# An attention and gated-MLP kernel on one core: the first pair of weight blocks is loaded behind the second unit's queries, keys and values

## The chip, the cores and the metric

The program runs on 1 core of one Trainium2 chip. The metric is device time in microseconds (us), the median of the runs of one kernel. Engines are named as in the profile: PE is the matrix engine, PEld its weight loads, DVE the vector engine, ACT the scalar engine, POOL the GpSimd engine, SP the engine that issues every DMA of this kernel.

## The reference, cut to what matters

```python
# attention inside chunks of 64 tokens; q, k, v are (8 batches, 8 heads, 576, 64)
scores = scale * q_c @ k_c.T;  attn = softmax(scores);  out = attn @ v_c
# the heads side by side give x: 4608 tokens x 512
xn  = x / sqrt(mean(x * x) + 1e-6) * rms_g
g   = xn @ w_gate                    # 512 -> 1536
val = xn @ w_val                     # 512 -> 1536
return (silu(g) * val) @ w_out       # 1536 -> 512
```

All arrays arrive as float32 in the reference; the three weights are handed to the kernel as 64-bit integer words of wider numbers and are turned into float32 on the chip.

## The kernel before

**Work.** Tokens are cut into 18 units of 256 (`UT`), two units to a token tile of 512 (`TT`), 9 tiles. Attention is done unit by unit, in two halves of 128 tokens each: scores (`scores`, L254), softmax on DVE and ACT (`softmax`, L267 to L271; `softmax_rows`, L288 to L303), a transpose of the probabilities on PE (`att_transpose`, L312, copied back by ACT in L313), the product with the values (`att_values`, L430) and the scaling by row sums and by the RMS (`norm`, L452, L440, L441, L443, L458). The normed rows are transposed on PE (L511) and split by ACT (L489) and DVE (L490) into a high and a low part, `xh` and `xl`, so that three matmuls with rounded operands make one product of float32 accuracy.

**Weights.** The hidden dimension is cut into 12 blocks, f0 to f11. The list `pairs` holds 18 loads of 1 MB, in the order up f0, up f1, out f0 and f1, up f2, up f3, out f2 and f3, and so on; here they are called block 0, block 1, block 2 and so on. An "up" load carries the gate and the value weights of one f, an "out" load the output weights of two. Each is loaded as raw 64-bit words (`conv_load`, L159) and converted: ACT takes the high words (L167) and the low words (L168); DVE clamps, shifts, merges and adds (L176, L177, L178, L181); ACT makes the rounded high half (L192), DVE the low half (L200), both in a tile `parts`; an up block is also stored as float32 (`wfd`, L194) when L181 is done. There are three working tiles `w` for this, so block 6 takes the tile of block 3 and waits for block 3's L200.

**Stages.** Units 0 and 1 are done first, with PE mostly waiting; then token tile 0 runs through the 12 blocks (L522 is the up product, `ps_g` and `ps_v`; L557 the product with the output weights, `acc`), while the 18 loads are converted under it and the attention of units 2 and 3 is put between. From the second tile on the weights are there, and in the last six tiles products of halves are combined with fewer matmuls (L736, L912).

**Order.** The order on each engine through the first token tile is not written out: the framework's scheduler chooses it, once, when the program is built, from the order in which the code calls things and from priorities. From the second tile on the order on PE is the one written. Each engine works through its list in order; a list entry that waits holds up all behind it. SP issues the DMAs in its own list order, and a DMA also waits until the one eight places ahead of it has landed. The PSUM pool `ps_a` has two banks: unit 2's scores take both (`ps_s_555`, `ps_s_556`), and the transposes of its probabilities (L312) need these banks again, so the first L312 waits until ACT has read all of the one bank and the second until it has read all of the other.

`load_first_unit` loads queries and keys of unit 0 in four pieces, `load_first_values` its values, `load_unit(1)` the queries, keys and values of unit 1 (L222 to L224). The call that the change moves is at L997:

Of the kernel before, what the change touches and what calls it, by code (L numbers as in the profile page):

```python
# [78 lines left out]
def tile_chunk_attn_swiglu(  # L79
# [76 lines left out]
    def conv_load(n):  # L156
        if n < len(pairs):
            kind, f = pairs[n]
            nc.sync.dma_start(raws[n], w_up[f] if kind == "up" else w_out[f // 2])  # L159
# [58 lines left out]
    def load_unit(u):  # L218
        qt = io.tile([P, NPAIR, UT], F32, tag="io", name="qt")
        kt = io.tile([P, NPAIR, UT], F32, tag="io", name="kt")  # L220
        vt = io.tile([P, NPAIR, UT // CH, D], F32, tag="io", name="vt")
        nc.sync.dma_start(qt, qT[u])  # L222
        nc.sync.dma_start(kt, kT[u])
        nc.sync.dma_start(vt, v[u])  # L224
        for s in range(2):
            state[2 * u + s] = {"q": qt, "k": kt, "v": vt}

    def load_first_unit():

        qt, kt = (x[:, 2 * i : 2 * i + 2].rearrange("p s (a t) -> p (s a) t", t=UT) for i in range(2))  # L230
        for s in range(2):
            part = slice(s * P, (s + 1) * P)
            nc.sync.dma_start(qt[:, :, part], qT[0][:, :, part])
            nc.sync.dma_start(kt[:, :, part], kT[0][:, :, part])
            state[s] = {"q": qt, "k": kt}

    def load_first_values():
        vt = io.tile([P, NPAIR, UT // CH, D], F32, tag="io", name="vt")
        nc.sync.dma_start(vt, v[0])
        for s in range(2):  # L240
            state[s]["v"] = vt
# [752 lines left out]
            self.n += 1  # L994

    load_first_unit()
    conv_load(0)  # L997
    load_first_values()
    load_unit(1)
    nc.sync.dma_start(g_col, rms_g)  # L1000
    for n in range(1, AHEAD):
        conv_load(n)
# [216 lines left out]
```

## Time and profile before

| | us |
|---|---|
| runs of the kernel | 924.17, 926.05, 926.56; median 926.05 |
| the profiled execution: its own time, and its span | 923.97, 922.2 |
| PE busy | 897.4 (97%) |
| DVE, ACT, POOL busy | 571.3, 449.3, 171.4 |
| first matmul of the first token tile | at 35.58 |

The span is the stretch from the first to the last recorded instruction. A row of the timeline gives the start, the duration, the engine, the line, what is written and read, and in brackets how long the engine had been idle before it and what ended that. Rows of one line that follow each other are merged, with their count behind x.

### The profile page before, as it was taken

The numbers are of one execution on the slowest core, as the hardware profiler recorded it, in microseconds if no ns is written. First come the engines' busy times: TensorE is split into PE (matmuls) and PEld (weight loads), VectorE is DVE, ScalarE is ACT, GpSimd is POOL, SyncE is SP. The second block draws the span as 40 slices with busy tenths as digits, with TensorE's granted clock in tenths as the row PEclk, the third lists the DMA queues.
The fourth block names the chain that finished last, engine by engine and source line by source line (L and its number), as shares of the span: only waits on it lengthen the run. The fifth ranks groups of instructions, "written<-read, shape, count | busy, mean of one in ns | idle before, by whom it ended". The sixth has DMA issues, their size and how long they took to land.

```text
span 922.2 us, 17497 instructions
## 1 busy us (share of the span) xinstructions
PE 897.4 (97%) x6900; PEld 735.5 (80%) x6900; DVE 571.3 (62%) x985; ACT 449.3 (49%) x721; POOL 171.4 (19%) x155
## 2 busy tenths in 40 slices
PE   5699999999999999999999999999999999999998
PEld 4578788888888788888878888888888888888886
DVE  5989975464546555864764735657555545544775
ACT  4989953463446553654444424546433332332352
POOL 0000002233200000233233002323330003432200
PEclk9999999999999999999999999999999999999999
DMA  8699899777975643888798788676997965785901
GB/s 336 263 331 345 320 347 347 244 264 230 306 275 148 185 150 114 310 283 298 231 352 309 283 332 318 219 261 224 328 332 260 343 241 182 284 298 191 354 24 68
DMA packets 101969, 242.84 MB, mean 263 GB/s; under 512 B 9344, under 2 KB 64128, under 8 KB 86912
## 3 DMA queue, kind: packets, MB, share of 16 engines
q1 hardware_dynamic: 101888, 241.74, 74.6%
q8 instruction: 54, 0.88, 0.4%
q14 instruction: 27, 0.22, 0.1%
HBM read 176.69 MB, written 65.01 MB: 262 GB/s over the span
## 4 chain that ended last, share of the span: by engine, by line
PE 84%; ACT 6%; DVE 5%; DMA 3%; issue 1%; SPq 1%; POOL 0%; ACTq 0%; DVEq 0%
PE acc L557 22%; PE ps_c L736 11%; PE ps_b L736 10%; PE ps_a L736 10%; PE ps_g L522 8%; PE ps_v L522 7%; PE ps_d L736 5%; PE ps_o L376 2%; PE ps_s L254 2%; PE ps_b L912 2%; PE ps_c L912 2%; PE ps_a L912 2%; DMA wr<-wsd 1%; ACT e L294 1%; PE ps_d L912 1%
## 5 line engine op out<-in xcount | busy, mean ns | idle before, releaser
L557 PE MATMUL acc<-wo,gh 128*128 128x512 f32 x384 | 118.5, 390 | 0.0
L736 PE MATMUL ps_c<-xp,wr 128*128 128x512 f32 x432 | 104.5, 391 | 0.2 <-DMA wr<-wsd 0.2
L736 PE MATMUL ps_b<-xp,wr 128*128 128x512 f32 x432 | 104.7, 391 | 0.0
L736 PE MATMUL ps_a<-xp,wr 128*128 128x512 f32 x432 | 103.5, 390 | 0.0
L522 PE MATMUL ps_g<-xh,parts 128*128 128x512 f32 x288 | 96.8, 396 | 0.3 <-ACT xh L489 0.3
L522 PE MATMUL ps_v<-xh,parts 128*128 128x512 f32 x288 | 95.1, 391 | 0.0
L736 PEld LDWEIGHTS ps_c<-xp,wr 128*128 128x128 f32 x432 | 80.7, 188 | 17.5 <-DMA wr<-wsd 0.7
L736 PEld LDWEIGHTS ps_a<-xp,wr 128*128 128x128 f32 x432 | 80.9, 188 | 16.9
L736 PEld LDWEIGHTS ps_b<-xp,wr 128*128 128x128 f32 x432 | 80.6, 188 | 17.1
L557 PE MATMUL acc<-parts,gh 128*128 128x512 f32 x288 | 90.2, 394 | 0.0
L809 POOL TENSOR_TENSOR g<-u,u 128x512 f32<-128x512 f32 x18 | 23.2, 1288 | 328.8 <-DVE u L805 270.2
L557 PEld LDWEIGHTS acc<-wo,gh 128*128 128x128 f32 x384 | 71.9, 188 | 15.0
L838 ACT CAST gh<-g 128x512 fp32r<-128x512 f32 x64 | 39.8, 623 | 80.6 <-PE acc L557 64.4
L839 DVE TENSOR_TENSOR gl<-g,gh 128x512 fp32r<-128x512 f32 x64 | 45.0, 706 | 54.9 <-ACT gh L838 54.8
L557 PE MATMUL acc<-wo,gl 128*128 128x512 f32 x192 | 75.0, 390 | 0.0
L522 PEld LDWEIGHTS ps_g<-xh,parts 128*128 128x128 f32 x288 | 54.1, 189 | 12.7 <-ACT xh L489 0.7
L522 PEld LDWEIGHTS ps_v<-xh,parts 128*128 128x128 f32 x288 | 54.5, 189 | 11.3
L557 PEld LDWEIGHTS acc<-parts,gh 128*128 128x128 f32 x288 | 53.3, 188 | 11.3
L544 DVE TENSOR_TENSOR sg<-ps_v,sg 128x512 f32<-128x512 f32 x36 | 24.7, 687 | 52.6 <-PE ps_v L522 40.4
L557 PE MATMUL acc<-parts,gl 128*128 128x512 f32 x144 | 56.4, 392 | 0.0
L522 PE MATMUL ps_v<-xl,parts 128*128 128x512 f32 x144 | 56.4, 392 | 0.0
L522 PE MATMUL ps_g<-xl,parts 128*128 128x512 f32 x144 | 56.3, 391 | 0.0
(165 smaller groups left out, 1593.2 us busy)
## 6 DMA issues: line engine op xcount, KB each, us to landing
wr<-wsd SPq DMA_DIRECT2D x63, 1024.0 KB, 8.9
wo<-wod SPq DMA_DIRECT2D x24, 1024.0 KB, 8.5
raw<-w_up_dram SPq DMA_DIRECT2D x12, 1024.0 KB, 8.1
vt<-v_dram SPq DMA_DIRECT2D x18, 512.0 KB, 6.9
wsd<-parts SPq DMA_DIRECT2D x18, 512.0 KB, 7.4
qt<-qT_dram SPq DMA_DIRECT2D x17, 512.0 KB, 5.8
kt<-kT_dram SPq DMA_DIRECT2D x17, 512.0 KB, 6.0
out_dram<-o SPq DMA_DIRECT2D x28, 256.0 KB, 2.3
```

The costliest lines, as they stand in the source:

```text
L254: nc.tensor.matmul(st["s"][j][c * CH : (c + 1) * CH, pr], st["q"][rows, pr, tok : tok + CH], st["k"][rows, pr, tok : tok + CH], start=True ...
L294: nc.scalar.activation(e[:, pr, j], st["s"][j][:, pr], AF.Exp, scale=SCALE, bias=mx[:, j, s, pr], accum_out=rs[:, s, pr, j],)
L376: nc.tensor.matmul(st["o"][(2 * c + t) * Q : (2 * c + t + 1) * Q, h * D : (h + 1) * D], eT[c][rows, t, h], vt[rows, c, h], start=True, sto ...
L522: nc.tensor.matmul(ps, a[f][:, cols], b[dt], start=(dt == 0 and i == 0), stop=(dt == NDT - 1 and i == 2),)
L544: nc.vector.tensor_tensor(sg, pv, sg, op=ALU.mult)
L557: nc.tensor.matmul(acc[s], a[:, cols], b, start=(f == 0 and i == 0), stop=(f == NF - 1 and i == 2),)
L736: nc.tensor.matmul(ps, w[:, a, m, cols], xp[:, b, kt], start=start and kt == 0 and i == 0, stop=stop and kt == 1 and i == 2, skip_group_ch ...
L809: nc.gpsimd.tensor_tensor(g[:, 0, 1], kp["u2"], kept[0]["u2"], op=mult)
L838: nc.scalar.copy(gh, src)
L839: nc.vector.tensor_tensor(gl, src, gh.bitcast(F32), op=ALU.subtract)
L912: nc.tensor.matmul(ps[m][INTO[p]], w[:, m, a], parts[c], start=p in FROM and i == 0 and k == 0, stop=p in LAST and i == NPR - 1 and k == 2 ...
```

## The change

One call is moved two lines down, behind `load_first_values()` and `load_unit(1)`:

```diff
     load_first_unit()
-    conv_load(0)
     load_first_values()
     load_unit(1)
+    conv_load(0)
     nc.sync.dma_start(g_col, rms_g)
     for n in range(1, AHEAD):
         conv_load(n)
```

On SP, at the start of the program, the load of block 0 (L159, `raw`) goes from the fifth DMA to the ninth:

```order
 L233 DMA x<-qT_dram 128x4x128
 L234 DMA x<-kT_dram 128x4x128
-L159 DMA raw<-w_up_dram 128x1024
 L239 DMA vt<-v_dram 128x1024
 L222 DMA qt<-qT_dram 128x1024
 L223 DMA kt<-kT_dram 128x1024
 L224 DMA vt<-v_dram 128x1024
+L159 DMA raw<-w_up_dram 128x1024
 L1000 DMA g_col<-rms_g_dram 128x4
 L159 DMA raw<-w_up_dram 128x1024
```

Four DMAs of 512 KB now stand ahead of that load. The scheduler answers by another order on PE, DVE, ACT and SP through the whole first token tile. On DVE, in the first unit's attention, three instructions of block 0's conversion (L176 to L178) stood between the softmax sums (L278) and the scaling of the first half (L452):

```order
-L176 TENSOR_SCALAR w<-w 128x1024
-L177 TENSOR_SCALAR w<-w 128x1024
-L178 SCALAR_TENSOR_TENSOR w<-raw,w 128x1024
 L452 TENSOR_TENSOR x<-ps_o_255,rs 128x4x2x32
 L452 TENSOR_TENSOR x<-ps_o_256,rs 128x4x2x32
-L181 ISA w<-raw,w 128x2048
```

They now follow behind the softmax reductions of unit 1, some seventeen rows further down the list.

Later on DVE, where unit 2's scores are reduced (L288) and block 3's low half is made (L200), the order before was:

```order
L181 ISA w<-raw,w 128x2048
L200 TENSOR_TENSOR parts<-w,parts 128x1024
L288 TENSOR_REDUCE mx_u<-ps_s_555 128x8
L544 TENSOR_TENSOR sg<-ps_v,sg 128x512
L288 TENSOR_REDUCE mx_u<-ps_s_556 128x8
```

and with the change it is:

```order
L181 ISA w<-raw,w 128x2048
L288 TENSOR_REDUCE mx_u<-ps_s_555 128x8
L288 TENSOR_REDUCE mx_u<-ps_s_556 128x8
L200 TENSOR_TENSOR parts<-w,parts 128x1024
L289 TENSOR_SCALAR mx_u<-mx_u 128x16
```

Block 3's low half now stands behind both reductions.

On ACT, in the softmax of unit 2 (L294, exponentials of `ps_s_555` and `ps_s_556`, 16 of them), two function tables are used in turn, one for L294 and one for the SiLU of the blocks (L540). From the first SiLU in that stretch (block f2) to block 5's high half (L192) the order before was:

```order
L540 ACT_TABLE_LOAD
L540 ACTIVATE sg<-ps_g 128x512
L294 ACT_TABLE_LOAD
L294 ACTIVATE e,rs_u<-ps_s_556,mx_u 128x64 x3
L545 CAST gh<-sg 128x512
L294 ACTIVATE e,rs_u<-ps_s_556,mx_u 128x64
L294 ACTIVATE e,rs_u<-ps_s_555,mx_u 128x64 x4
L294 ACTIVATE e,rs_u<-ps_s_556,mx_u 128x64 x4
L192 CAST parts<-w 128x1024
```

and with the change, from behind the first SiLU on, it is:

```order
L294 ACTIVATE e,rs_u<-ps_s_555,mx_u 128x64
L545 CAST gh<-sg 128x512
L294 ACTIVATE e,rs_u<-ps_s_555,mx_u 128x64 x2
L294 ACTIVATE e,rs_u<-ps_s_556,mx_u 128x64 x4
L294 ACTIVATE e,rs_u<-ps_s_555,mx_u 128x64 x4
L540 ACT_TABLE_LOAD
L540 ACTIVATE sg<-ps_g 128x512
L294 ACT_TABLE_LOAD
L294 ACTIVATE e,rs_u<-ps_s_556,mx_u 128x64 x2
L545 CAST gh<-sg 128x512
L294 ACTIVATE e,rs_u<-ps_s_556,mx_u 128x64 x2
L192 CAST parts<-w 128x1024
```

A second SiLU (block f3), with a table load on either side, now stands inside the softmax, ahead of the last four exponentials and of block 5's high half. On PE the second L312 of unit 2 moves from the middle of f3's products to behind them.

## Rows read from the trace of the kernel before

**Rows 1.** The page, busy time of PE, share, instructions.
```profile
PE 897.4 (97%) x6900; PEld 735.5 (80%) x6900; DVE 571.3 (62%) x985; ACT 449.3 (49%) x721; POOL 171.4 (19%) x155
```
**Rows 2.** Waits of PE over the span: us in total, times, longest.
```profile
PE ps_s L254 <- DMA x<-kT_dram: 6.7, 2, 5.0
...
PE ps_o L376 <- DMA eT<-away_e: 1.6, 2, 1.4
...
PE ps_t L312 <- ACT e L294: 1.0, 2, 0.5
```
**Rows 3.** Busy time by stretch: length, then each engine, clock granted, DMA.
```profile
50.00:75.00 25.00, 24.49 (x169) 19.83 (x168) 22.58 (x31) 23.45 (x54) 0.00 (x0) 1.00 0.95 336
75.00:125.00 50.00, 49.48 (x335) 39.99 (x334) 48.85 (x67) 44.98 (x83) 3.62 (x2) 1.00 0.92 336
```
**Rows 4.** DMA issues from 0 to 5.5 us: KB, us to landing.
```profile
raw<-w_up_dram SPq DMA_DIRECT2D x1, 1024.0 KB, 7.2
...
kt<-kT_dram SPq DMA_DIRECT2D x1, 512.0 KB, 9.5
```
**Rows 5.** Timeline of SP at the start.
```profile
3.44 0.62 SPq L159 DMA_DIRECT2D raw<-w_up_dram  x1
...
5.05 0.74 SPq L223 DMA_DIRECT2D kt<-kT_dram  x1
```
**Rows 6.** Timeline of all engines, first unit.
```profile
12.18 0.69 DVE L176 TENSOR_SCALAR w<-w 128x1024 f32<-128x1024 f32 x1
...
12.68 1.14 PE L430 MATMUL ps_o<-vt,eT 64*64 64x64 f32 x32 [0.40 <-ACT eT L313]
...
13.63 1.23 DVE L178 SCALAR_TENSOR_TENSOR w<-raw,w 128x1024 int32<-128x1024 int32 x1
14.78 0.75 DVE L452 TENSOR_TENSOR x<-ps_o,rs 128x256 f32<-128x256 f32 x2
15.34 0.55 PE L430 MATMUL ps_o<-vt,eT 64*64 64x64 f32 x5 [1.53 <-DVE x L452]
```
**Rows 7.** Timeline of all engines, end of the first two units.
```profile
29.02 0.55 POOL L443 TENSOR_TENSOR ri<-ss,mhalf 128x1 f32<-128x1 f32 x1 [9.13 <-DVE ss L441]
...
32.07 1.29 POOL L443 TENSOR_TENSOR ri<-ss,mhalf 128x1 f32<-128x1 f32 x1 [2.50 <-DVE ss L441]
...
33.40 0.72 ACT L458 ACTIVATE x<-x,ri 128x512 f32<-128x512 f32 x1
...
35.58 0.79 PE L522 MATMUL ps_g<-xh,parts 128*128 128x512 f32 x1 [0.29 <-ACT xh L489]
```
**Rows 8.** Timeline of DVE, block 3's low half and unit 2's scores.
```profile
49.01 1.21 DVE L200 TENSOR_TENSOR parts<-w,parts 128x1024 fp32r<-128x1024 f32 x1
50.15 0.68 DVE L288 TENSOR_REDUCE mx_u<-ps_s 128x8 f32<-128x512 f32 x1
```
**Rows 9.** Timeline of ACT, softmax of unit 2.
```profile
50.26 1.14 ACT L167 ACTIVATE w<-raw 128x1024 f32<-128x1024 f32 x1
...
53.38 1.28 ACT L294 ACT_TABLE_LOAD   x1 [1.31 <-DVE mx_u L289]
...
55.99 1.28 ACT L540 ACT_TABLE_LOAD   x1
57.28 0.60 ACT L540 ACTIVATE sg<-ps_g 128x512 f32<-128x512 f32 x1
...
63.20 1.11 ACT L192 CAST parts<-w 128x1024 fp32r<-128x1024 f32 x1
```
**Rows 10.** Timeline of PE, units 2 and 3 in the first token tile.
```profile
62.24 0.66 PE L312 MATMUL ps_t<-ident,e 128*128 128x128 f32 x4 [0.51 <-ACT e L294]
...
67.59 0.62 PE L557 MATMUL acc<-parts,gh 128*128 128x512 f32 x2
...
72.02 0.39 PE L522 MATMUL ps_g<-xh,parts 128*128 128x512 f32 x1
...
106.30 0.66 PE L312 MATMUL ps_t<-ident,e 128*128 128x128 f32 x4 [0.52 <-ACT e L294]
```

## The prediction

> **What bounds the kernel now.** I read the page first: PE is busy for 897.4 of 922.2 us [rows 1]. Next the waits of PE over the whole span: the large ones lie ahead of the first token tile, where PE waits for the first queries and keys; after that the longest is 1.4 us in all the rest, and the transposes of the probabilities (L312) wait for ACT's exponentials twice, 0.5 us each [rows 2]. So from 35.58 us, the first matmul of the first token tile [rows 7], PE goes nearly without a gap to the end. The time is the moment at which this dense run starts, plus the matmuls, which the change does not touch, plus the waits inside the run. Then busy time by stretch, to see which engine could make such waits: between 50 and 125 us DVE is busy 22.58 of 25 and 48.85 of 50 us, ACT 23.45 of 25 and 44.98 of 50 [rows 3]. There the weights are converted under the matmuls, with almost nothing to spare. Work that these two engines do later than before stays late until the conversion is over. That is the side on which the change can lose; the first 35 us are the side on which it can win.
>
> **The transfers.** Nothing is added or removed; one load of 1 MB passes four of 512 KB on SP's queue. Before, block 0 is issued at 3.44 and lands 7.2 us later, at 10.64; the keys of unit 1 are issued at 5.05 and land after 9.5, at 14.55 [rows 4, 5]. Three loads of 512 KB lie between these two landings, 1.5 MB in 3.9 us, so 2.6 us per MB. Unit 1's keys gain the 1 MB that went ahead and land at about 11.9; block 0 has 2 MB more ahead of it and lands at about 15.8. The loads behind are ahead of the same bytes as before: 0.
>
> **The first two units.** Before, PE finished the first half's values at 12.68 + 1.14 = 13.82, but the scaling L452 began only at 14.78, since DVE was busy from 12.18 with block 0's clamp, shift and merge (L176 to L178); unit 1's scores stood on PE behind a matmul that waited 1.53 us for that L452 [rows 6]. Without block 0 on DVE L452 can follow the values at once: 1.0 us earlier, and some 1.4 if ACT's copy of the probabilities, which had ACT's L167 ahead of it, comes earlier too. The keys at 11.9 are then no hindrance. Little of this survives: block 0's two ACT instructions (1.1 us each, as the L167 of [rows 9]) and its DVE instructions, which had filled waits before, now stand between here and the dense run, in front of unit 1's own work. One of the two on ACT takes most of the 1.4; I keep 0.35 us at the last squares, an estimate. A second piece comes from POOL. Its power for the RMS took 0.55 us at 29.02 and 1.29 us at 32.07, where DVE ran L176 and L177 beside it, and the last scaling L458 waited for it until 33.40 [rows 7]. In the new order DVE has L178 there. At 0.55 us this gives 0.74 more. I take the dense run 1.1 us earlier, at 34.5; the ends are 0.35 and 1.4.
>
> [...] No row here shows POOL beside L178, and 1.29 against 0.55 only shows that something on DVE blocks it.
>
> **The converter falls behind.** By the order, DVE had done three L178 and two L200 when it came to the second unit's low parts (L490); now it has done two and one. That is 1.23 + 1.21 = 2.4 us of work [rows 6, 8] that now lies under the dense run. It starts 1.1 us earlier, so the conversion is 1.3 us late on the clock. Then block 3's low half (L200, which ended at 50.2) has two reductions of 0.68 us ahead of it that stood behind it: 50.2 + 1.3 + 1.4 = 52.9 [rows 8]. PE waited for nothing here before, and wants this half at about 52.5 now: a wait between 0 and 1.0 us, I take 0.45.
>
> **Unit 2's softmax.** ACT's first instruction on block 6 (L167) began at 50.26, at the end of that L200, since block 6 takes block 3's working tile [rows 8, 9]; it now starts at about 53.0. What is queued behind it on ACT is the whole softmax of unit 2. From that L167 to block 5's L192 it was 63.20 - 50.26 = 12.9 us; the wait of 1.31 us in it goes, since the reductions now come first; and a SiLU with two table loads comes in, 1.28 + 0.60 + 1.28 = 3.2 us [rows 9]. So L192 begins, and the last exponential ends, at 53.0 + 12.9 - 1.3 + 3.2 = 67.8, 4.6 us later than before. The second L312 on PE waits for that exponential. It now stands behind block f3, whose products ended at 67.59 with both L312 and a wait of 0.51 in them [rows 10]: 67.59 - 0.65 (the lead left) - 0.5 - 0.4 (one L312) = 66.0. PE waits 1.8 us in place of 0.5. Behind it come the products with block 5, which want its high half (67.8 + 1.1) and its low half (another 1.2): 70.1, with about 1 us of matmuls done in between. Before, those products and the values of unit 2 took 72.02 - 67.59 = 4.4 us [rows 10]; f4 starts at 70.1 + 3.4 = 73.5, against 72.02: 1.5 us late.
>
> [...]
>
> **Unit 3's softmax.** ACT and DVE have no room to recover [rows 3], so ACT is still about 4.6 us late there and PE 1.5. Before, PE already waited 0.52 us at 106.30 [rows 10]. If the transposes stood where they were, PE would lose the other 3.1 us; but both now stand behind all products of the block before, and the first of them needs only one bank's exponentials. Between 0 and 3.1 I take 1.0, as most of the difference is covered by these products. Behind that the blocks' weights are ahead of PE again.
>
> **The sum**, as lag against the profiled execution: start -1.1, block 3 +0.45, the transpose of unit 2 +1.3, block 5 +0.85, unit 3 +1.0: **+2.5 us**. That is 926.5 on the profile's own 923.97; the median of the runs lies 2.1 us above that execution, so I forecast 926.05 + 2.5 = **928.5**. With the ends of all terms: no new wait and the full lead, -1.4, or 924.6; the least lead and the larger waits, about +5, or 931.
>
> **Rivals.**
> - *The lead survives.* If ACT reaches the SiLU of f3 as soon as its products are done, the transposes wait no more than now, and only the earlier start counts: -1.1, **924.9**, not slower. For it: the 1.53 us wait of PE and DVE's block 0 ahead of L452 are plain in the rows [rows 6], and what I lose comes from a chain of small lags. Against it: ACT has 3.2 us more ahead of the last exponentials, whatever the lag, and it decides as soon as more than 0.5 us of the wait is left. It falls at the second L312 of unit 2. Chance 0.20.
> - *More is lost.* POOL's power stays at 1.29 us, so that the run starts at 35.2, and unit 3's wait is nearer 3 than 1: 2.5 + 0.7 + 1.3 = +4.5, **930.5**. For it: DVE busy 48.85 of 50 us [rows 3]. Against it: PE, itself late, asks later. Chance 0.20.
> - *Nothing that counts.* The conversion had margin that I don't see, the waits only change places, and the start gives back what they cost: **926.0**. For it: before, PE waits in the whole tile only for the two transposes. Chance 0.15. A change that doesn't do what it says is excluded by the order on SP.
>
> **Numbers.** The forecast has 0.45. About 0.3%, 2.8 us, is what a measurement of this kernel can tell from no change: faster is below 923.3, slower above 928.8. Of the forecast, with an error of some 1.2 us, four tenths lie above; of the second rival nearly all. Slower 0.40, same 0.54, faster 0.06. The range is 924.5 to 931.0; the forecast's own is 927 to 930.
>
> **What will show it.** Right: L452 of the first half near 13.4 us; the first L522 near 34.5; a wait of PE for block 3's L200 near 53; a wait of PE for L294 of 1 to 2 us near 67; f4 near 73.5. Wrong: no wait of PE over 0.6 us between 35 and 125 us, or a first L522 at 35.5 or later; both upset the sum, the one downwards, the other upwards.

## The result, and the profile after

| | before | after |
|---|---|---|
| runs beside each other | 923.92 to 926.56, median 924.2 (5 runs) | 928.59 to 930.83, median 929.54 (5 runs) |
| profiled execution, and its span | 923.97, 922.2 | 928.81, 927.0 |
| f0, f4 and f9 start on PE (first L522) | 35.58, 72.02, 117.97 | 34.49, 75.77, 122.75 |

The changed kernel takes 1.005 times as long, 95% interval 1.0034 to 1.0065: **slower by about 5 us**. The forecast was +2.5 us, 928.5, with a range of 924.5 to 931.0. It was reckoned from 926.05, and the runs beside it had 924.2: the time came out 1.0 us from the forecast, but the change, +5.3, is more than double the +2.5.

The page of after, busy time of each engine [rows 1]:

```profile
PE 899.9 (97%) x6900; PEld 736.2 (79%) x6900; DVE 570.1 (61%) x985; ACT 452.2 (49%) x723; POOL 170.3 (18%) x155
```

The waits of PE over the span of after (in total, times, longest) [rows 2]:

```profile
PE ps_t L312 <- ACT e L294: 3.5, 2, 2.1
...
PE ps_g L522 <- DVE parts L200: 0.4, 1, 0.4
...
PE acc L557 <- ACT parts L192: 0.3, 1, 0.3
```

The transposes, which waited 1.0 us in all, wait 3.5, and two waits for halves of converted weights are new. Busy time by stretch in after [rows 3] (PE, PEld, DVE, ACT, POOL, then the clock granted to PE, the share of the DMA engines, GB/s):

```profile
35.50:50.00 14.50, 14.50 (x116) 11.68 (x114) 13.71 (x18) 12.77 (x16) 0.00 (x0) 0.87 0.76 269
50.00:75.00 25.00, 22.19 (x157) 17.06 (x150) 19.43 (x26) 21.90 (x51) 0.00 (x0) 0.93 0.99 359
75.00:125.00 50.00, 48.56 (x348) 39.25 (x339) 47.14 (x62) 45.97 (x82) 1.61 (x1) 1.00 0.91 319
```

Between 50 and 75 us PE stands still for 2.8 us, and DVE, one of the two full engines there, now has 5.6 us to spare: it waits too. The clock is below 1.00 twice. Where the time was lost is in PE's own rows of after, from block 3 to f9 [rows 10]:

```profile
53.97 0.74 PE L522 MATMUL ps_g<-xh,parts 128*128 128x512 f32 x2 [0.42 <-DVE parts L200]
...
69.11 0.66 PE L312 MATMUL ps_t<-ident,e 128*128 128x128 f32 x4 [2.10 <-ACT e L294]
70.05 2.50 PE L557 MATMUL acc<-parts,gh 128*128 128x512 f32 x5 [0.28 <-ACT parts L192]
72.34 0.63 PE L557 MATMUL acc<-parts,gl 128*128 128x512 f32 x1
72.77 0.63 PE L557 MATMUL acc<-parts,gh 128*128 128x512 f32 x1
73.20 0.50 PE L557 MATMUL acc<-parts,gl 128*128 128x512 f32 x1
73.54 0.39 PE L557 MATMUL acc<-parts,gh 128*128 128x512 f32 x1
...
111.35 0.66 PE L312 MATMUL ps_t<-ident,e 128*128 128x128 f32 x4 [1.44 <-ACT e L294]
```

Behind the wait of 2.10 us products come about 0.43 us apart, eight steps in 3.49 us from 70.05 to 73.54, not 0.227 as elsewhere; the clock granted to PE from 70 to 72 us is 0.50. At 0.227 they would have taken 1.82, so 1.67 us went there. And ACT's rows in unit 2's softmax in after [rows 9]:

```profile
54.00 1.16 ACT L167 ACTIVATE w<-raw 128x1024 f32<-128x1024 f32 x1 [1.33 <-DVE mx_u L289]
55.17 1.28 ACT L294 ACT_TABLE_LOAD   x1
...
56.90 1.28 ACT L540 ACT_TABLE_LOAD   x1
...
58.80 1.28 ACT L294 ACT_TABLE_LOAD   x1
...
64.00 1.28 ACT L540 ACT_TABLE_LOAD   x1
65.29 0.60 ACT L540 ACTIVATE sg<-ps_g 128x512 f32<-128x512 f32 x1
65.91 1.28 ACT L294 ACT_TABLE_LOAD   x1
...
68.95 1.04 ACT L192 CAST parts<-w 128x1024 fp32r<-128x1024 f32 x1
```

Five table loads where there were three: a second SiLU, at 65.29, splits the 16 exponentials again, and block 5's L192 begins at 68.95, not at 63.20.

The lag against before, from the two profiled executions: dense run -1.09; its first 4.8 us with matmuls 0.43 apart, where before it was 3.5 us, +0.67 (eleven matmuls on, the lead is 0.42); L200 +0.42; L312 2.10 - 0.51 = +1.6; L192 +0.28; the low clock +1.67. That makes 3.55; f4 is 3.75 late. From f4 to f9 1.03 more, at unit 3. After that nothing counts: the spans differ by 4.8. At the head of the dense run I go by the spacing: the granted clock reads 0.50 there in after (35 to 38 us), but 1.00 in before, where the matmuls come 0.43 apart as well.

### The profile page after: what moved, and what is told of

The parts are those of the page before. It is cut to its first block, busy times and chain, and to the rows that moved or that the text cites. A ratio compares the mean times of both kernels' runs of the same rounds, so it can differ in the third digit from the quotient of the medians.

```text
span 927.0 us, 17502 instructions
## 1 busy us (share of the span) xinstructions
PE 899.9 (97%) x6900; PEld 736.2 (79%) x6900; DVE 570.1 (61%) x985; ACT 452.2 (49%) x723; POOL 170.3 (18%) x155
## 4 chain that ended last, share of the span: by engine, by line
PE 86%; ACT 5%; DMA 3%; DVE 3%; issue 1%; POOL 1%; SPq 1%; DVEq 0%; POOLq 0%
PE acc L557 23%; PE ps_c L736 11%; PE ps_b L736 10%; PE ps_a L736 10%; PE ps_g L522 9%; PE ps_v L522 8%; PE ps_d L736 5%; PE ps_o L376 2%; PE ps_b L912 2%; PE ps_c L912 2%; PE ps_a L912 2%; PE ps_s L254 2%; DMA wr<-wsd 1%; ACT e L294 1%; PE ps_d L912 1%
## 5 line engine op out<-in xcount | busy, mean ns | idle before, releaser
L522 PE MATMUL ps_g<-xh,parts 128*128 128x512 f32 x288 | 97.0, 397 | 0.7 <-DVE parts L200 0.4
L522 PE MATMUL ps_v<-xh,parts 128*128 128x512 f32 x288 | 95.5, 392 | 0.0
L736 PEld LDWEIGHTS ps_c<-xp,wr 128*128 128x128 f32 x432 | 80.7, 188 | 17.9 <-DMA wr<-wsd 1.0
L522 PEld LDWEIGHTS ps_g<-xh,parts 128*128 128x128 f32 x288 | 54.6, 190 | 13.5 <-DVE parts L200 0.8
L557 PEld LDWEIGHTS acc<-parts,gh 128*128 128x128 f32 x288 | 54.0, 191 | 11.9 <-ACT parts L192 0.5
L522 PEld LDWEIGHTS ps_v<-xh,parts 128*128 128x128 f32 x288 | 54.4, 189 | 11.2
L522 PE MATMUL ps_g<-xl,parts 128*128 128x512 f32 x144 | 56.6, 393 | 0.0
L522 PE MATMUL ps_v<-xl,parts 128*128 128x512 f32 x144 | 56.3, 391 | 0.0
```

Of the source, the lines that this page charges most:

```text
L522: nc.tensor.matmul(ps, a[f][:, cols], b[dt], start=(dt == 0 and i == 0), stop=(dt == NDT - 1 and i == 2),)
L557: nc.tensor.matmul(acc[s], a[:, cols], b, start=(f == 0 and i == 0), stop=(f == NF - 1 and i == 2),)
L736: nc.tensor.matmul(ps, w[:, a, m, cols], xp[:, b, kt], start=start and kt == 0 and i == 0, stop=stop and kt == 1 and i == 2, skip_group_ch ...
```

## The experiments

The theory: the moved load makes ACT break unit 2's softmax twice, PE waits for it, and the wait lowers PE's clock. The rivals: the conversion is simply late, by the later landing of block 0; or only the transposes stand in the way. Since every edit also changes the order that the scheduler chooses, each run is read by stages of its profile as well: f1 to f4 holds unit 2's softmax, f4 to f9 unit 3's. The ratio is to the kernel before on the same chip. f0 is the start of the first up product of the dense run, the other columns are the time between such starts.

| kernel | median | ratio, 95% | f0 | f0 to f1 | f1 to f4 | f4 to f9 |
|---|---|---|---|---|---|---|
| before | 923.05 to 924.2 in four sets | 1 | 35.58 | 7.12 | 29.32 | 45.95 |
| after | 929.54 | 1.0034 to 1.0065 | 34.49 | 7.83 | 33.45 | 46.98 |
| e12 after, second time | 928.84 | 1.0046 to 1.0078 | 34.38 | 7.60 | 33.35 | 47.01 |
| e1 after, softmax whole | 922.49 | 0.9973 to 0.9991 | 34.88 | 6.96 | 30.74 | 45.49 |
| e6 the same, unit 2 alone | 924.28 | 0.9989 to 1.0016 | 35.77 | 7.29 | 30.56 | 46.08 |
| e11 as e1, with a copy on DVE | 923.42 | 0.9992 to 1.0010 | 35.30 | 7.65 | 30.57 | 44.96 |
| e5 before, softmax whole | 928.25 | 1.0033 to 1.0072 | 35.17 | 7.07 | 28.69 | 52.06 |
| e10 as e5, with the copy | 925.55 | 1.0011 to 1.0038 | 35.75 | 7.45 | 28.39 | 48.91 |
| e2 half of the move | 932.29 | 1.0072 to 1.0100 | 36.55 | 8.03 | 29.65 | 52.19 |
| e9 as e2, with the copy | 927.33 | 1.0031 to 1.0056 | 36.40 | 8.01 | 29.61 | 48.70 |
| e8 as e2, softmax whole | 923.74 | 0.9987 to 1.0018 | 36.75 | 8.01 | 29.60 | 44.34 |
| e3 after, transposes later | 931.09 | 1.0061 to 1.0088 | 34.50 | 6.96 | 31.04 | 49.50 |
| e4 after, waits ahead of f0 filled | 934.23 | 1.0095 to 1.0134 | 34.68 | 7.11 | 33.10 | 47.33 |
| e7 after, wait of 2.1 us filled | 938.24 | 1.0130 to 1.0180 | 34.30 | 7.69 | 35.20 | 47.79 |

The first block, f0 to f1, differs between executions of one order (after, e12, e1, e6, e11, e3 and e7 do not differ up to there, nor do before, e5 and e10): it holds the end of the spacing of 0.43, which came sooner or later (at 39.1 us in before, 39.3 in after). The start differs too, and most of that is the landing of unit 0's second keys. In before and in after:

```profile
7.87 1.13 PE L254 MATMUL ps_s<-x 64*64 64x64 f32 x32 [1.72 <-DMA x<-kT_dram]
```

```profile
7.36 1.13 PE L254 MATMUL ps_s<-x 64*64 64x64 f32 x32 [0.93 <-DMA x<-kT_dram]
```

In e6 these scores began at 8.82. Counted from them, the dense run begins 27.7 to 27.9 us later in the three executions with the order of before, and 26.9 to 27.3 in the seven with the order of after. So the order is worth about 0.8 us of lead, and 0.51 of the 1.09 us is the landing in this pair of executions.

**e1: the softmax kept whole.**

```diff
-                    nc.scalar.activation(
+                    with urgent(): nc.scalar.activation(
                         e[:, pr, j],
```

> The changed kernel, with the exponentials of softmax_rows (units 2 and 3) given the same high priority as the SiLU, so that on ACT all 16 stand together and no SiLU with two table loads comes between them. Theory (the broken softmax on ACT makes the wait, and the wait lowers the clock): from the L167 of block 6 at 54.0, with one table load and 16 exponentials of 0.29 us, the last ends near 61.3 and not at 69.1; the wait of 2.10 us for L294 shrinks below 0.7, block 5's L192 begins near 64 and not at 68.95. The SiLU is now behind the softmax, so PE may wait for its bank, some 1.5 us. No stretch of L557 at 0.43 us (1.7 us) and less of unit 3's 1.44. Together 926.0 to 928.0 against 929.5. Rival (the conversion is simply late, whatever ACT's order): block 5's L192 and PE's wait stay where they are, 929 to 930.

922.49 us, 0.9982 times the kernel before: by the ratios 6.3 us less than after, and below the 926 to 928 expected. ACT's and PE's rows in unit 2's softmax:

```profile
54.86 1.28 ACT L294 ACT_TABLE_LOAD   x1
...
60.76 1.09 PE L312 MATMUL ps_t<-ident,e 128*128 128x128 f32 x8 [0.21 <-ACT e L294]
61.02 1.28 ACT L540 ACT_TABLE_LOAD   x1
62.32 0.60 ACT L540 ACTIVATE sg<-ps_g 128x512 f32<-128x512 f32 x1
62.81 1.04 ACT L192 CAST parts<-w 128x1024 fp32r<-128x1024 f32 x1
62.97 0.50 PE L522 MATMUL ps_g<-xh,parts 128*128 128x512 f32 x1 [1.11 <-ACT sg L540]
```

One table load up to the last exponential, not five; L192 at 62.81, not at 68.95; in place of the 2.10 us a wait of 0.21, and the 1.11 for the SiLU that was foreseen. No product behind it is slow: the granted clock is 1.00 from 50 to 75 us. As the cause of this wait the conversion that was "simply late" is refuted: the edit raised ACT's exponentials alone (the scheduler's orders on DVE and PE changed with it, from 59 us on), and the load is where the change put it. Whether lateness costs something besides is asked at e10 and e11.

**e6: unit 2 alone** (`tc.high_priority(offset=URGENT * (u == 2))` at the same place).

> The changed kernel, with the exponentials of unit 2 alone at high priority; unit 3 as in the changed kernel. Theory (the lateness of unit 3 is handed on from unit 2): no wait over 0.5 us for L294 at unit 2, f4 near 72.6 as in e1_soft, and unit 3's wait of 1.44 us falls below 0.7 without an edit of its own: 922.3 to 923.5. Rival (unit 3 is late by itself, by its own broken softmax): 1 to 2 us more than e1_soft, 923.5 to 925.

L312 waits 0.23 us at unit 2 and 0.78 at unit 3, where no edit was made and after had 1.44. About half of unit 3's wait was handed on from unit 2, half is its own; f4 to f9 is 0.6 us longer than in e1, the ratio 0.2% higher. Both sides are partly right.

**e3: transposes one block later** (`f in (3, 8)` and `(4, 9)` in place of `(2, 7)` and `(3, 8)`).

> The changed kernel, with the transposes and the values of units 2 and 3 one block of f later in the program (blocks 3 and 4, 8 and 9 instead of 2 and 3, 7 and 8). Theory (the exponentials on ACT are late, and block 5's L192, queued behind them, with them): PE no longer waits 2.1 us at L312, but as long at the products with block 5, which wait for L192 until 69 to 70; the time stays at 928.5 to 930. Rival (only the transposes are in PE's way): the 2.1 us, the half clock behind it (1.7) and unit 3's 1.44 go, 924 to 926.

931.09 us, ratio 1.0074 (1.0061 to 1.0088): no gain, as the theory had it, but not in its manner. The scheduler put all eight transposes where the second four had stood, ahead of the products with block 5, and PE waited there as before:

```profile
68.35 0.66 PE L312 MATMUL ps_t<-ident,e 128*128 128x128 f32 x4 [2.35 <-ACT e L294]
69.28 1.76 PE L557 MATMUL acc<-parts,gh 128*128 128x512 f32 x5 [0.28 <-ACT parts L192]
70.88 0.40 PE L557 MATMUL acc<-parts,gl 128*128 128x512 f32 x1
71.11 0.40 PE L557 MATMUL acc<-parts,gh 128*128 128x512 f32 x1
```

So whether PE would have waited for L192 instead isn't shown. It shows something else: here PE had waited 2.35 us and the granted clock stayed at 1.00. The ninth product begins 2.29 us after the first, in after 3.49: by this pair the low clock costs 1.2 us, by the spacing 1.67. The total hides that the stages moved both ways: f1 to f4 took 31.04 us, 2.4 less than in after, and f4 to f9 took 49.50, 2.5 more. There unit 3's L312 waited 2.42 us, and behind it the granted clock was 0.50 (111.9 to 115.2 us). So at unit 2 the rival was nearer than the total says.

**e12: after, once more**, unedited.

> The changed kernel itself, timed and profiled beside the others. Theory: 928.5 to 930 as before; a wait of 2.1 us at unit 2's second L312 and 1.4 at unit 3's, in any execution, as they come from the order on ACT. The clock behind that wait, and the moment at which it rises in the dense run, may differ from execution to execution, which gives its price: where it stays at 1.00 the matmuls behind the wait come 0.23 us apart and f4 starts 1.7 us sooner. Rival (the low clock belongs to the order too): 0.43 apart again.

928.84 us, ratio 1.0062. The waits are nearly the same, 2.10 and 1.48 us (1.44 in after), and the clock fell again: granted 0.86 from 70 to 80 us, the products 0.43 apart. The rival held: with this order the low clock came with the wait, in both executions.

**e4 and e7: filling PE's waits.** In e4 16 transposes more ahead of the dense run (`for n in range(8 * (u == 1 and s == half))`), in e7 20 more ahead of unit 2's second L312.

> The changed kernel, with 16 more transposes on PE (their results are overwritten) in its two waits of 2.4 and 2.2 us before the dense run. Theory (the first 4.2 us of the dense run go at half the clock because PE had been waiting): the matmuls of the first token tile come 0.23 us apart from the start or after 1 us at most, not 0.43 until 38.5; 1.6 to 2.1 us less, so 927.4 to 927.9, if the later waits of PE don't take it back; if they do (PE asks earlier for the same halves) 929 to 929.5 and a longer wait near 53 or 67. Rival (the spacing of 0.43 comes from the data, not from the clock): no change of the spacing, 929.5.

> The changed kernel, with 20 transposes of the first half's probabilities (overwritten by the real ones) on PE in the wait of 2.1 us ahead of unit 2's second L312. The wait itself stays. Theory (behind the wait PE runs at half the clock for some 3.5 us, 8 matmuls at 0.43 instead of 0.23 us, which costs 1.7 us): the matmuls behind come 0.23 apart, 927.5 to 928.3. Rival (the spacing of 0.43 has another cause, or the next wait takes the gain back): 929 to 930.

Both failed as tests of the total: 934.23 and 938.24 us. In e4 waits of 0.55, 1.25 and 0.73 us were left, and f0 took 7.11 us, no less than the 6.96 of e1 without such transposes. In e7 the added transposes waited for the same exponential as the real ones, and then ran in PE's way, 20 of them in 3.80 us, with a granted clock of 0.85 from 70 to 80 us:

```profile
68.76 3.80 PE L311 MATMUL ps_t<-ident,e 128*128 128x128 f32 x20 [2.10 <-ACT e L294]
```

The rest of both losses lies much later, where neither kernel was edited: in each, two waits that the profile ascribes to nothing. In e4, and in e7:

```profile
407.45 2.56 PE L736 MATMUL ps_d<-xp,wr 128*128 128x512 f32 x10 [1.91 <-issue]
...
471.66 2.29 PE L736 MATMUL ps_b<-xp,wr 128*128 128x512 f32 x5 [2.47 <-issue]
```

```profile
409.55 0.27 PE L376 MATMUL ps_o<-vt,eT 64*32 64x64 f32 x2 [2.67 <-issue]
...
476.14 3.50 PE L736 MATMUL ps_b<-xp,wr 128*128 128x512 f32 x8 [3.22 <-issue]
```

What they wait for stays open, and with it the price of the clock from a run of its own.

**e2: half of the move.**

```diff
     load_first_values()
+    conv_load(0)
     load_unit(1)
-    conv_load(0)
```

> Block 0 is loaded between unit 0's values and unit 1's loads: half of the move. In its order ACT has one SiLU, not two, inside unit 2's softmax, as in the kernel before, and block 0 is late by 0.5 MB, not by 2 MB. Theory (ACT's order in unit 2's softmax decides): the dense run starts between 34.5 and 35.6, the waits for L294 are below 0.8 us each, no half clock at 70 to 74: 924 to 925.5, as before. Rival (every MB ahead of block 0 delays the conversion, and this costs): about a quarter of the loss of 5.3 us stays at least, 925.5 to 927.

932.29 us: slower than after, and neither theory nor rival had it. The dense run began at 36.55, not between 34.5 and 35.6, and in e9 and e8, with the load at the same place, at 36.40 and 36.75; why half of the move starts later than either kernel was not followed up. Unit 2 went as the theory said, with no wait for L294 at all. But then, in e2, at unit 2's norm:

```profile
84.66 0.16 DVE L478 TENSOR_SCALAR ss_u<-ss_u 128x2 f32<-128x2 f32 x1
84.73 1.22 DVE L200 TENSOR_TENSOR parts<-w,parts 128x1024 fp32r<-128x1024 f32 x1
84.90 4.48 POOL L480 TENSOR_TENSOR ri_u<-ss_u,mhalf 128x2 f32<-128x2 f32 x1 [50.57 <-DVE ss_u L478]
...
87.60 1.22 DVE L181 CUSTOM_DVE_ANT_0 w<-raw,w 128x2048 uint16<-128x2048 uint16 x1
...
89.41 0.72 ACT L482 ACTIVATE x<-x,ri_u 128x512 f32<-128x512 f32 x1 [4.05 <-POOL ri_u L480]
...
94.27 0.50 PE L522 MATMUL ps_g<-xh,parts 128*128 128x512 f32 x1 [2.21 <-ACT parts L192]
...
97.78 1.22 PE L522 MATMUL ps_g<-xh,parts 128*128 128x512 f32 x2 [2.78 <-DVE parts L200]
```

A power of 256 numbers on POOL took 4.48 us. DVE ran four instructions without a gap until 88.82, and POOL ended 0.56 us later, about what a power of 128x1 took at 29.02 in before (0.55 [rows 7]). ACT stood behind it for 4.05 us, and the weights behind ACT were late for PE twice. Behind these two waits the granted clock was 0.53 from 95 to 102 us.

**e9: DVE waits for POOL.** The same kernel, with one copy on DVE:

```diff
         nc.gpsimd.tensor_tensor(ri, ss, mhalf.broadcast_to([P, 2]), op=ALU.pow)
+        with urgent(): nc.vector.tensor_copy(ss, ri)
+        ri = ss
```

> The kernel of e2_half, with one more instruction on DVE: a copy of POOL's power (L480's result, 128x2), one DVE instruction behind L478, which ACT then reads. DVE must wait for POOL there, and so leaves off for about 0.6 us; DVE's order around it is that of e2_half. Theory (POOL's power gets on only when DVE pauses: 4.48 us in e2_half, of which 4.2 beside a DVE without a gap): L480 takes one L200 and its own 0.55, 1.8 us at most, ACT's wait of 4.05 falls below 1.5, PE's waits of 2.2 and 2.8 us near 94 to 98 go: 924 to 927 against 932.3. Rival (L480 is slow for another reason, or the conversion is behind anyway): 930 to 933.

927.33 us, 5 us less (4 by the ratios), just above the 924 to 927 of the theory. DVE's order around it is the same but for the copy (the lines behind it are one or two higher):

```profile
84.51 1.22 DVE L200 TENSOR_TENSOR parts<-w,parts 128x1024 fp32r<-128x1024 f32 x1
84.68 1.61 POOL L480 TENSOR_TENSOR ri_u<-ss_u,mhalf 128x2 f32<-128x2 f32 x1 [50.49 <-DVE ss_u L478]
...
86.32 0.17 DVE L481 COPY ss_u<-ri_u 128x2 f32<-128x2 f32 x1 [0.59 <-POOL ri_u L480]
...
86.58 1.34 ACT L484 ACTIVATE x<-x,ss_u 128x512 f32<-128x512 f32 x2 [0.86 <-DVE ss_u L481]
...
95.22 0.73 PE L523 MATMUL ps_g<-xh,parts 128*128 128x512 f32 x2 [2.01 <-DVE parts L200]
```

DVE gave up 0.59 us, POOL took 1.61, ACT's wait fell to 0.86. One of PE's two waits is left, with the clock at 0.50 behind it (96.7 to 100 us). So POOL explains 4 to 5 of the 8 us that e2 lost, the waits and the low clock that followed from it included.

**e8: half of the move, softmax whole** (the edits of e2 and e1).

> The kernel of e2_half (block 0 between unit 0's values and unit 1's loads), with the exponentials of units 2 and 3 at high priority. In e2_half POOL's power for unit 2 (L480) took 4.48 us beside DVE's L200, L178, L176, L181, ACT waited 4.05 us for it, and PE 2.2 and 2.8 us near 94 to 98 for the weights behind. Theory (that stall of POOL beside a busy DVE is what made e2_half slow): if the order changes so that L480 takes under 2 us, no wait of PE over 1 us is left between 75 and 125 and the time is 923 to 926; if L480 again takes over 4 us, it stays over 929. Rival (the place of the load itself is bad, POOL or not): over 928 with a short L480.

923.74 us, and L480 took 1.15 us both times: the first branch of the theory. The rival fell: the place of the load alone does not make e2 slow.

**e5: the control**, the edit of e1 in the kernel before.

> The kernel before, with the same high priority for the exponentials of units 2 and 3 as in e1_soft: the control. Theory (the moved load makes ACT break unit 2's softmax twice instead of once, and that is nearly the whole loss): before, PE waited only 0.51 and 0.52 us at its transposes, so no more than about 1 us is to be had here, and the SiLU behind the softmax may cost up to 0.5: 923.2 to 924.5. Then e1_soft (922.5) would be 0.7 to 2 us faster than this one, which is the earlier start. Rival (keeping the exponentials together helps any order by several us, and says nothing on the change): 918 to 921.

928.25 us: outside both. From f1 to f4 it gained 0.6 us, as the theory said. But L480 took 5.08 us (78.44 to 83.52), and PE waited later for a SiLU and for a low half, in e5:

```profile
98.44 0.50 PE L522 MATMUL ps_g<-xh,parts 128*128 128x512 f32 x1 [1.55 <-ACT sg L540]
...
112.42 0.74 PE L522 MATMUL ps_g<-xh,parts 128*128 128x512 f32 x2 [2.47 <-DVE parts L200]
```

**e10 and e11: the pair with the copy**, before and after, both with the softmax whole.

> The control once more: the kernel before with the exponentials kept together (e5_soft_before), and DVE's copy of POOL's power as in e9_half_copy, since L480 took 5.08 us in e5_soft_before (78.44 to 83.52) and hid what the first edit does. Theory: L480 under 2 us, no wait of PE over 1 us between 75 and 125. Up to f4 e5_soft_before was 1.3 us ahead of the kernel before, e1_soft 0.6 behind it; so this one should come out 1 to 2 us faster than e1_soft (922.5): 920.5 to 922. Rival (with the exponentials together the changed order of loads is a gain): 922.5 to 924.

> The changed kernel with the exponentials kept together (e1_soft) and the copy of POOL's power; L480 took only 1.15 us in e1_soft. Theory: nothing to gain, 922 to 923.5; against e10_soft_before_copy it is the pure effect of the moved load with neither the table loads nor POOL's stall in the way: 0.5 to 2 us slower. Rival: 0.7 to 1.1 us faster, the earlier start of the dense run.

In e10 L480 takes 1.60 us at most and the wait of 1.55 is gone, but one of 2.45 for L200 stays, at 109.9: 925.55. e11 is 923.42, no better than e1, as expected. So in total the moved load came out faster here, 1.0001 against 1.0024, where I had expected it 0.5 to 2 us slower. Up to f4 the expectation held: 71.59 in e10, 73.52 in e11. What turned it round is the wait for L200 in unit 3's stage of e10, with the granted clock at 0.50 behind it (111.5 to 114.8 us). I take it for another chance of the order; no run tests that.

What is shown: from f1 to f4 the change costs 4.1 us (33.4 against 29.3). With the softmax whole it costs 2.1 (30.6, the mean of e1, e6 and e11, against 28.5, the mean of e5 and e10). So half of it hangs on the second break, with its wait and the clock behind it; the other half is there without it, and lies mostly in e1's 0.42 for L200 and 1.11 for the SiLU; that both are the converter's lag is argued from the rows and not tested. Not shown: what the later landing of block 0 costs with every engine's order as before, as no run holds the order fixed. **e1 has the lowest ratio of all kernels tried**, 0.9 to 2.7 per mille below the kernel before; e11, the same with a copy that had nothing to gain, came to 0.8 below to 1.0 above, so little of that is sure.

## Why the prediction was half right

- *The bound, and the two sides.* Right: PE from the first L522 to the end, the gain ahead of it, the loss in the conversion at 50 to 125 us.
- *The transfers.* Unit 1's keys landed at 12.7 us (11.9 foreseen) and block 0 at about 17.9 (15.8 foreseen), with ACT's first instruction on it at 18.35.
- *The start.* The dense run begins at 34.49 (34.5 foreseen), but that it fits so well is luck: executions of the same order began at 34.30 to 35.77, and the pieces are not those of the sum. L452 was earlier than foreseen, 12.86 against 13.4, and the part from POOL did not come. The rows of after, where I had expected 0.55 us [rows 7]:

```profile
30.42 1.23 DVE L178 SCALAR_TENSOR_TENSOR w<-raw,w 128x1024 int32<-128x1024 int32 x1
30.58 1.71 POOL L443 TENSOR_TENSOR ri<-ss,mhalf 128x1 f32<-128x1 f32 x1 [2.24 <-DVE ss L441]
...
32.32 0.72 ACT L458 ACTIVATE x<-x,ri 128x512 f32<-128x512 f32 x1 [0.98 <-POOL ri L443]
```

  The power took 1.71 us and ended 0.64 us after L178. So the lead was there ahead of POOL: the last squares (L440) begin at 29.59, before at 30.75, 1.16 us earlier where I had kept 0.35. Of the two values that I had for the power, 0.55 and 1.29 us, the longer was the nearer, where I had given 0.55 the preference. And I was wrong that no row of before shows POOL beside L178. One does, where an L178 runs from 81.22 to 82.44; POOL's power took 1.70 us there, and that could have settled the choice:

```profile
81.39 1.70 POOL L480 TENSOR_TENSOR ri_u<-ss_u,mhalf 128x2 f32<-128x2 f32 x1 [48.03 <-DVE ss_u L478]
```

- *Block 3.* 0.45 foreseen near 53, 0.42 at 53.97. The size is luck in part: L200 ended at 53.9, not 52.9, since the L181 ahead of it was 2.5 us late (50.37 against 47.88) and not 1.3, and PE came 1 us later than foreseen as well, at 53.55.
- *Unit 2's softmax.* Foreseen: one SiLU with two table loads more inside it, a wait of 1.8 near 67; measured 2.10, up to 69.11, since block 6's L167 began at 54.00 and not at 53.0. e1 shows it as a cause. The table load at 64.00 took 1.28 us and the SiLU began at 65.29; in before the SiLU began at 57.28 behind the load of 55.99, also of 1.28 [rows 9].
- *Block 5.* This is the step that failed. I had 0.85 us of waits for its halves and the matmuls at their usual spacing. The wait was 0.28; in its place came eight products at a granted clock of 0.50, 1.67 us by the spacing, in e12 1.58. The sum had no term for the clock at all, though in the kernel before the matmuls at the head of the dense run were 0.43 apart too. There the profiled execution of after lost 0.67 more, since the spacing of 0.43 ended at 39.3, before at 39.1, in spite of the earlier start; but that part is the execution's, as e1 and e3 ran the same block in 6.96 us and not in 7.83. Together 2.3 us: f4 at 75.77 against 73.5 foreseen, +4.8 between the profiled executions against +2.5 in the sum. The median of 929.54 lies nearer to 928.5 than that because the forecast started from 926.05, 1.85 us above the runs of before that stood beside it.
- *Unit 3.* 1.0 foreseen, a choice between 0 and 3.1, and 1.03 measured between f4 and f9.
- *The rivals.* "More is lost" has the nearest number, 930.5, and was right that POOL's power would not shorten; but the run began at 34.49 and not at 35.2, and unit 3 cost 1.0 and not 2.3. Its number came true by the clock, which it did not name. "The lead survives" fell at the place that I gave for it, and "nothing that counts" with the 5 us.

## What to carry to other kernels

Where one engine runs dense to the end, ask of each new wait not only how long it is but what PE's clock does behind it: here a wait of 2.1 us cost 1.2 to 1.7 more. Where a scheduler chooses the order, a load moved by two lines is a new program: look on ACT for a function that comes between calls of another (here each break brought two table loads of 1.28 us), and on POOL for a short instruction beside a crowded DVE (here a power took 1.15 us in e1 and 5.08 in e5). Keeping such runs together by priority paid in both kernels with a moved load (e1 and e8), but in the kernel before it did not: e5 and e10 came out 0.5% and 0.2% slower, by waits that the new order brought elsewhere. So read the stages of each new order, not the total alone.

## Not expected of the hardware

- POOL's power of 128x2 numbers took 1.15 us in e1 and e8, 4.48 in e2 and 5.08 in e5, in the last two ending 0.56 us after the last of a row of DVE instructions without a gap. In those rows it did not end beside one of them. With a pause of 0.59 us on DVE it took 1.61 (e9). It can end without one: in after it took 1.61 us, from 85.15 to 86.76, and ended 0.56 us after an L200 while the L178 behind it was running (86.11 to 87.33), and in before it ended 0.64 us after an L178, beside the L176 that followed. Which DVE instructions lengthen it, and when it ends beside one, isn't settled.
- In the first token tile the granted clock fell behind the wait of 2.10 us in after (0.50 from 70 to 72 us), e12 (0.86 from 70 to 80) and e7 (0.85 from 70 to 80), and behind 2.01 to 2.78 us in e9, e3 at unit 3, e10 (0.50 in each), e5 (0.91 from 100 to 120) and e2 (0.53). It stayed at 1.00 behind the 2.35 us of e3 at unit 2, and behind 1.70 us in e7 (80 to 100). Why e3's 2.35 us went without it stays open.
- The dense run of one order began at 34.30 to 35.77 us, mostly by the landing of the first keys, and its first block took 6.96 to 7.83 us: a single profile tells these to no better than that.
